# Two decode layers on one Trainium2 core: gate and up as rows, mean taken off late, joint score steps of two kv heads, w_down in six loads, new orders

## The chip, the cores and the metric

The kernel runs on one core of a Trainium2 chip. A core has a matrix engine (TensorE; PE in the profile, PEld where it loads weights), a vector engine (VectorE, DVE), a scalar engine (ScalarE, ACT), GpSimd (POOL) and SyncE (SP), which here only issues transfers. Each engine runs its own instruction list in order and waits on semaphores. Operands lie in SBUF (128 partitions), matmul results in eight banks of PSUM. 16 DMA engines fetch from HBM. The metric is the device time of one execution in microseconds (us), taken as the median of several; less is better.

## The reference

One pass over four tokens (B = 4, one position each) computes attention, feed-forward, attention, feed-forward, and both layers use the same weights and the same K and V cache:

```python
x = A_x                                                        # [4, 1, 448]
x = x + _A_ref(_layernorm(x), A_k_cache, A_v_cache, A_wq, A_wo)
x = x + _B_ref(_layernorm(x), B_w_gate, B_w_up, B_w_down)
x = x + _A_ref(_layernorm(x), A_k_cache, A_v_cache, A_wq, A_wo)
x = x + _B_ref(_layernorm(x), B_w_gate, B_w_up, B_w_down)

# _A_ref: 16 query heads, 8 kv heads, head size 256, the last W = 2048 of 8192 keys
q = (x @ wq).reshape(B, 1, 16, 256).transpose(0, 2, 1, 3)
scores = einsum("bhqd,bhkd->bhqk", q, k) * 256 ** -0.5
out = (softmax(scores) @ v).transpose(0, 2, 1, 3).reshape(B, 1, 4096) @ wo
# _B_ref: 448 -> 1792 -> 448
out = (silu(x @ w_gate) * (x @ w_up)) @ w_down
```

All data are bf16. The window of one token and kv head is 1 MB of K and 1 MB of V (2048 x 256), so the cache that is read measures 4 x 8 x 2 MB = 64 MB for one layer; the weights are 12.2 MB.

## The kernel before, in words

**Recording and orders.** `build()` records every operation into a graph (`g.op`, `g.dma`), with its engine, its emitting function, and the names it reads and writes. The order on each engine doesn't follow from this recording: it is written out in lists of operation numbers, `SEQ_PE`, `SEQ_DVE`, `SEQ_ACT`, `SEQ_POOL` and `SEQ_SP` (a "w" in SEQ_PE is a filler matmul that computes nothing needed, L1214). `schedule()` applies the lists and places the semaphore waits that the dependencies need.

**Loads.** All loads stand on SP's queue in the order of SEQ_SP. K and V arrive in halves of 512 KB (a pair of K halves can be one load of 1024 KB); `SLOTS` gives each half one of 31 places in SBUF, with seven more in the space of wq after the last q projection. A load whose place is still in use waits on SP for the PE operation that last reads the place, and everything behind it on SP waits too. Of a token's eight heads, six K and six V are held in their places from layer 0 to layer 1 (`KEEP_K`, `KEEP_V`) and not loaded again. L942 and L944 issue K, L958 issues V, L555 issues weights.

**Groups.** `PLAN` lists the work in steps; "202+203" is a group of two kv heads, heads 2 and 3 of token 2 in layer 0 (token, layer, head). A group runs over the engines: DVE transposes each K half (L948); PE makes the scores of both heads (L982); DVE takes the maximum (L995); PE spreads it (L1000, L1003); ACT takes exp (L1013); PE turns the probabilities (L1026) and ACT copies them (L1035); PE sums them (L1043); PE multiplies by V (PV, L1057, four operations of eight matmuls for the two heads and two V halves); POOL (L1070), ACT (L1072) and DVE (L1074) scale; PE flips the result (L1080) and DVE writes it to one of two buffers `oT` (L1090). The output projection with wo adds each head's part in PSUM, as rows (L1110) or, for the last heads of a token, as columns (L1102). Three steps of PLAN hold two groups, four heads ("002+003 004+005"): with two oT buffers, heads 2 and 3 of such a step are overwritten by 4 and 5 before their out projection.

**Hand-over of a token.** After a token's eight heads of layer 0, its rows are copied and turned (ACT L857, DVE L859, PE L867), the residual is added (L849, L877), and `norm()` gathers the mean and the variance (L586, L599, with DVE L589, L604, L606 and a chain of small POOL operations up to L622). `ffn()` computes gate and up (L785) as columns: 14 x 4 blocks of 128 x 128 of each weight matrix stand in PE, and x is broadcast to 32 columns, so each takes 56 matmuls. Then come tanh (ACT L805), three DVE operations (L808, L810, L817) and down (L826, 56 matmuls). After the second residual and a second norm, `qproj()` makes q of layer 1 (L671, 32 matmuls), ACT scales and copies (L677), PE turns (L687), DVE expands (L694), PE spreads (L701), DVE copies to qc (L706) and POOL makes the group's stationary operand qe (L987). Then the scores of layer 1 for the held heads can run, after them their PV; these free the places that SP waits for. A token in `LATE` or `QLATE` (only token 3 before) starts gate, or the q projection, from the raw x, and its mean is taken off afterwards by a matmul with the weights' column sums (L800, or in the turn).

## Time and profile before

| what | value |
|---|---|
| three runs: lowest, median, highest | 283.07, 284.09, 286.08 us |
| profiled execution: span | 283.0 us |
| around the span | the median is 1.1 us above the span |
| PE busy | 210.4 us (74%) |
| DVE busy | 168.6 us (60%) |
| POOL, ACT busy | 77.2 us (27%), 50.9 us (18%) |
| HBM read | 96.05 MB |
| mean granted TensorE clock | 0.895 |

In the profile's rows L12 is line 12 of the kernel. A row of a timeline gives start, busy time, engine, line, operation, what is written and read, and the number of instructions; in brackets the idle time before it and what ended it. A row of waits gives the waiting engine and line, the releaser, the total, the number and the longest. The slices cut the span into 40 equal parts.

### The profile page before, as it was taken

Reading aid. Unit: us, or ns where it says so; the run is one execution under the profiler, and the core shown is the slowest. Engines: PE = TensorE matmul, PEld = TensorE weight load, DVE = VectorE, ACT = ScalarE, POOL = GpSimd, SP = SyncE. Lnnn points to the kernel's source line nnn. Section 1 sums busy time; section 2 is a strip of 40 time slices with the busy share of each in tenths; the row PEclk is TensorE's granted clock in tenths of the full one; section 3 lists DMA queues with packets and bytes.
Section 4 is the critical chain, followed back from the end, with each engine's and each line's share of the span. In section 5 each row is a group of like instructions: output and inputs, shape, how many; then the busy total and the mean of one; then the engine's idle time right before and its main releaser. Section 6 shows DMA issues by size and latency. Waiting matters only on the chain.

```text
span 283.0 us, 9526 instructions
## 1 busy us (share of the span) xinstructions
PE 210.4 (74%) x4204; PEld 120.8 (43%) x4204; DVE 168.6 (60%) x511; ACT 50.9 (18%) x123; POOL 77.2 (27%) x202
## 2 busy tenths in 40 slices
...
DMA  6999999999999999968799999948799997899300
GB/s 258 424 414 401 413 410 402 407 401 406 377 390 408 400 408 406 409 278 307 290 324 403 411 406 408 397 170 295 254 316 412 415 405 266 286 341 415 125 2 3
DMA packets 27752, 96.67 MB, mean 342 GB/s; under 512 B 2747, under 2 KB 6847, under 8 KB 26431
## 3 DMA queue, kind: packets, MB, share of 16 engines
...
q8 instruction: 33, 0.54, 0.8%
...
q10 hardware_dynamic: 8, 0.00, 0.0%
HBM read 96.05 MB, written 0.00 MB: 339 GB/s over the span
## 4 chain that ended last, share of the span: by engine, by line
DMA 30%; PE 27%; SPq 23%; DVE 12%; issue 3%; ACT 3%; POOL 0%
DMA half<-in_A_k_cache_dram 13%; DMA half<-in_A_v_cache_dram 11%; SPq L555 10%; DVE half L948 8%; SPq L958 8%; DMA wd_sb<-in_B_w_down_dram 6%; PE A L1214 5%; PE Y L1057 5%; PE S L982 4%; PE Z L785 3%; SPq L944 3%; SPq L942 3%; PE Z L826 2%; PE A L1110 2%; DVE oh L1074 1%
## 5 line engine op out<-in xcount | busy, mean ns | idle before, releaser
L948 DVE STREAM_TRANSPOSE half<-half 128x1024 uint32<-128x1024 uint32 x80 | 98.0, 1233 | 16.3 <-DMA half<-in_A_k_cache_dram 15.9
L1214 PE MATMUL A<-identb,small 128*128 128x512 bf16 x147 | 51.0, 452 | 7.4 <-DVE A L478 5.5
L1070 POOL TENSOR_TENSOR small<-small 128x4 f32<-128x4 f32 x32 | 32.4, 1015 | 68.0 <-DVE small L1048 61.7
L982 PE MATMUL S<-half,qe 128*8 128x256 bf16 (+1 forms) x1040 | 40.8, 305 | 12.0 <-DVE half L948 11.1
L1057 PE MATMUL Y<-half,pT 128*8 128x256 bf16 x1024 | 42.2, 296 | 7.3 <-DMA half<-in_A_v_cache_dram 3.9
L982 PEld LDWEIGHTS S<-half,qe 128*8 128x8 bf16 x1040 | 25.4, 92 | 26.1 <-DVE half L948 15.5
L987 POOL TENSOR_TENSOR qe<-qc,tiny 128x64 bf16<-128x64 bf16 x64 | 17.2, 292 | 60.1 <-PE S L982 46.4
L1013 ACT ACTIVATE praw<-S,small 104x256 bf16<-104x256 f32 x32 | 15.1, 473 | 81.7 <-DVE small L1009 81.2
L1057 PEld LDWEIGHTS Y<-half,pT 128*8 128x8 bf16 x1024 | 22.2, 90 | 17.8 <-DMA half<-in_A_v_cache_dram 5.3
L995 DVE TENSOR_REDUCE tiny<-S 104x1 bf16<-104x256 f32 x32 | 13.3, 418 | 19.0 <-PE S L982 19.0
L1072 ACT ACTIVATE oh<-Y 128x256 bf16<-128x256 f32 x32 | 12.3, 383 | 66.3 <-PE Y L1057 61.9
L1214 PEld LDWEIGHTS A<-identb,small 128*128 128x128 bf16 x147 | 13.0, 109 | 20.4 <-issue 7.4
L1074 DVE SCALAR_TENSOR_TENSOR oh<-oh,small,Y 128x256 bf16<-128x256 bf16 x32 | 15.0, 468 | 11.0 <-ACT oh L1072 10.4
L1110 PE MATMUL A<-wo_sb,oT 128*4 128x448 bf16 x220 | 17.2, 380 | 0.8 <-DVE oT L1090 0.6
L1080 PE MATMUL Y<-tiny,oh 128*128 128x4 bf16 x64 | 6.6, 172 | 15.1 <-DVE oh L1074 15.0
L1048 DVE TENSOR_REDUCE small<-Y 128x4 f32<-128x64 f32 x32 | 7.0, 218 | 13.8 <-PE Y L1043 12.1
L1026 PE MATMUL Y<-selt,praw 104*64 104x48 bf16 x256 | 10.1, 197 | 5.9 <-ACT praw L1013 5.5
L1080 PEld LDWEIGHTS Y<-tiny,oh 128*128 128x128 bf16 x64 | 4.2, 103 | 22.5 <-DVE oh L1074 19.6
L1035 ACT ACTIVATE pT<-Y 128x192 bf16<-128x192 f32 x32 | 10.5, 329 | 15.6 <-PE Y L1026 15.3
L1026 PEld LDWEIGHTS Y<-selt,praw 104*64 104x64 bf16 x256 | 6.7, 113 | 12.6 <-ACT praw L1013 9.9
L671 PE MATMUL Z<-half,xn 128*5 128x512 bf16 x160 | 10.2, 379 | 2.2 <-DVE st L606 0.8
L612 POOL TENSOR_SCALAR st<-st 128x1 f32<-128x1 f32 x16 | 4.4, 274 | 26.4 <-DVE st L606 26.4
(125 smaller groups left out, 219.7 us busy)
## 6 DMA issues: line engine op xcount, KB each, us to landing
half<-in_A_v_cache_dram SPq DMA_DIRECT2D x80, 512.0 KB, 12.1
...
wg_sb<-in_B_w_gate_dram SPq DMA_DIRECT2D x1, 1344.0 KB, 17.3
...
```

Source lines behind the costliest of these rows:

```text
L555: g.dma(rank, nbytes, lambda e: e.dma_start(dst, src), f"w{nw[0]}", w=key if isinstance(key, tuple) else (key,), run=run)
L948: return e.transpose(a, a)
L958: g.dma(pp + VLAG, 1 << 19, lambda e, cell=cell, hv=hv, vsrc=vsrc: e.dma_start(unit(cell), vsrc[hv]), None, w=(f"v{t}_{kvh}_{hv}",), run=4 ...
L982: last = e.matmul(Sb[s_][qd:qd + 8, c0:c0 + rhs.free_size()], lhsT=qe[q_][:, P, ce, :, :].rearrange("p a n -> p (a n)"), rhs=rhs, start=(c ...
L987: g.op(POOL, 0.25, pos - SLEAD - 1, lambda e, P=P, t=t, kvh=kvh: e.tensor_tensor(qe[q_][:, P, :, :, :], qc[t][:, kvh, :, :].unsqueeze(2).b ...
L1013: return e.activation(praw[0:R, 0:128 * n].rearrange("p (g r l) -> p g r l", g=2 * n, l=2), Sb[s_][0:R, 0:128 * n].rearrange("p (l g r) -> ...
L1026: last = e.matmul(Yb[p_][64 * h:64 * h + 64, c0:c0 + (48 if n == 2 else 32)], lhsT=praw[0:R, 64 * gg:64 * gg + 64], rhs=w, start=(gg == 0) ...
L1057: last = e.matmul(Yb[p_][32 * gg:32 * gg + M, 256:512], lhsT=pT[pt][:, gg, 2 * a + hv, 4 * P:4 * P + M] if n == 2 else p1[:, gg % 2, 2 * a ...
L1070: g.op(POOL, 0.69, pos, lambda e: e.tensor_tensor(ri[p_][:, 0:2 * n], rs[p_][:, 0:2 * n], expo[:, 1:1 + 2 * n], op=ALU.pow), r=(f"rs{p_}", ...
L1074: g.op(DVE, 0.43, pos, lambda e: e.scalar_tensor_tensor(out=oh[:, :], in0=oh[:, :], scalar=lomask[:, 0:1], in1=Yb[p_][:, 256:512], op0=ALU ...
L1110: last = e.matmul(Ab[32 * k:32 * k + B, 0:D], lhsT=oT[oi][:, k % 2, k // 2, :], rhs=wo_sb[:, 4 * kvh + k, :], start=False, stop=False, ski ...
L1214: return e.matmul(Ab[:, 0:512], lhsT=zero[:, 0:1].broadcast_to([128, 128]), rhs=identb[:, :].unsqueeze(1).broadcast_to([128, 4, 128]), sta ...
```

## The change

Parts of the change:

1. **Gate and up as rows.** x (one or two columns) now stands in PE and the weights move: 16 matmuls per matrix with 448 weight columns each, in four column groups of 32 rows. The rows of gate are copied out of PSUM by ACT (448 columns), those of up by ACT and DVE (224 each), and five small matmuls per matrix turn them back to columns. The hidden units stand in a new order, and w_down is loaded to match.
2. **Mean off late** for tokens 1, 2 and 3, in gate and up and in q. The scale of q moves from ACT's copy to the DVE operation that expands.
3. **Direct qe.** Where a token's first layer-1 group follows its q projection with nothing between in that PSUM bank (in the new order tokens 0 and 2), DVE makes qe straight from it, instead of the copy to qc and POOL's product.
4. **Steps of two heads.** The three steps of four heads become two steps each, so heads are no longer overwritten. Code for a group of one head, and its seven small DVE operations at the start, goes, as do an unused row form of the whole FFN.
5. **w_down in six loads** (four of 128 x 3 x 448, two of 128 x 448), 1568 KB together as before.
6. **New orders.** All five SEQ lists and SLOTS are replaced. SP issues the same bytes. PE has 113 fillers, 147 before. Scores stay one operation for both heads.

```diff
-ROWF = ()
-LATE = ((3, 0),)
-QLATE = (3,)
+LATE = ((1, 0), (2, 0), (3, 0))
+QLATE = (1, 2, 3)
+PRE = (0, 1, 2)
 PLAN = (
-    "000+001", "002+003 004+005", "006+007", "100+101", "012+013", "014+015", "016+017", "102+103", "104+105",
+    "000+001", "002+003", "004+005", "006+007", "100+101", "012+013", "014+015", "016+017", "102+103", "104+105",
     "106+107", "200+201", "010+011", "115+113", "116+112", "114+117", "202+203", "204+205", "206+207", "300+301",
-    "212+213 214+215", "216+217 302+303", "306+305", "304+307", "110+111", "210+211 316+313", "314+315",
+    "212+213", "214+215", "216+217", "302+303", "306+305", "304+307", "110+111", "210+211", "316+313", "314+315",
     "312+317", "310+311",
 )
 SEQ_PE = (
-    "53 w w 57 w w w 60 w w w 68 w w 71 79 w 82 w 90 w w 93 w w 103 106 104 107 109 110 112 w w w w w 138 140 w w w w "
...
+    "46 50 53 61 64 w 72 75 83 86 96 99 97 100 102 103 w 105 136 173 138 175 141 210 143 w 212 178 145 180 341 146 247 "
...
-            load(rank_d, 1605632, wd_sb[:, :, :], B_w_down.rearrange("(c p) n -> p c n", p=128), "wd", 430)
+            for j in range(4):
+                load(rank_d, 344064, wd_sb[:, 3 * j:3 * j + 3, :], B_w_down[448 * j:448 * j + 384, :].rearrange("(c p) n -> p c n", p=128),
+                     f"wd{j}", 430)
+            wd_e = B_w_down.rearrange("(x h q) n -> x h q n", x=2, h=2)
+            for x in range(2):
+                load(rank_d, 114688, wd_sb[:, 12 + x, :], wd_e[x, :, 384:448, :], f"wd{4 + x}", 430)
...
+            if one:
+                vec(rank, lambda e: e.scalar_tensor_tensor(
+                    out=qS[:, 0:128].rearrange("p (c y) -> p c y", c=4),
+                    in0=Zb[:, 0:32].unsqueeze(1).broadcast_to([128, 4, 32]), scalar=st[:, ts[0], 8:9],
+                    in1=qone[:, :].unsqueeze(2).broadcast_to([128, 4, 32]), op0=ALU.mult, op1=ALU.mult),
+                    ("z", "qone", f"st{ts[0]}r2"), ("wa",), 0.25, ("Z",))
...
                 for cc in range(c0, c1):
-                    for fc in range(NFC):
+                    for j in range(4):
                         if cc < 3:
-                            lhsT, x = w[:, cc * FF + fc * 128:cc * FF + fc * 128 + 128], xn[:, cc, sl]
+                            lhsT, c = xn[:, cc, sl], cc * FF + 448 * j
                         else:
-                            lhsT = w[:, 3 * FF + (fc % 7) * 128:3 * FF + (fc % 7) * 128 + 128]
-                            x = xe[:, fc // 7, sl]
-                        last = e.matmul((Zb, Z2)[gi][:, k * m * fc:k * m * fc + k * m], lhsT=lhsT,
-                                        rhs=x.unsqueeze(2).broadcast_to([128, k, m]),
-                                        start=(fc == 0 and cc == 0), stop=(cc == 3), skip_group_check=True)
+                            lhsT, c = xe[:, j // 2, sl], 3 * FF + 448 * (j % 2)
+                        last = e.matmul(zb[32 * j:32 * j + k, 0:448], lhsT=lhsT, rhs=w[:, c:c + 448],
+                                        start=(cc == 0), stop=(cc == 3), skip_group_check=True)
+                return last
+
+            def turn(e, gi):
+                last, src = None, 512 * gi
+                o = zbs[gi][:, 0:NFC * k].rearrange("p (f t) -> p f t", t=k)
+                for c in range(4):
+                    for h in ((0,), (0, 1))[c == 3]:
+                        w_, f0, st_ = (128, c, 3) if c < 3 else (64, 12, 1)
+                        js = slice(0, 4) if c < 3 else slice(h, 4, 2)
+                        f1 = f0 + (10 if c < 3 else 2)
+                        last = e.matmul(o[64 * h:64 * h + w_, f0:f1:st_, :],
+                                        lhsT=wideb[:, src + 128 * c:src + 128 * c + w_], rhs=idn[:, js, 0:k],
+                                        start=(c == 0), stop=True, skip_group_check=True)
...
+            g.op(SCA, 0.54, rank, lambda e: e.activation(wideb[:, 0:448], Zb[:, 0:448], ACT.Copy), r=("z",), w=("wa",), bank=("Z",))
+            g.op(PE, 0.16, rank, lambda e: turn(e, 0), r=("wa", "identb"), w=("z",), bank=("Z",))
+            g.op(SCA, 0.31, rank, lambda e: e.activation(wideb[:, 512:736], Z2[:, 0:224], ACT.Copy), r=("z2",), w=("wb",), bank=("Z2",))
+            vec(rank, lambda e: e.tensor_copy(wideb[:, 736:960], Z2[:, 224:448]), ("z2",), ("wb2",), 0.31, ("Z2",))
+            g.op(PE, 0.16, rank, lambda e: turn(e, 1), r=("wb", "wb2", "identb"), w=("z2",), bank=("Z2",))
...
+                if t in PRE and layer == 1 and ahead[t][0] == gi and fresh[0] == (t, g.writer["z2"]):
+                    vec(pos, lambda e, P=P, kvh=kvh: e.tensor_tensor(
+                        qe[q_][:, P, :, :, :],
+                        Z2[:, 16 * kvh:16 * kvh + 16].rearrange("p (c h) -> p c h", h=2).unsqueeze(2).broadcast_to([128, 8, 4, 2]),
+                        qmask[:, :].unsqueeze(1).unsqueeze(3).broadcast_to([128, 8, 4, 2]), op=ALU.mult),
```

On PE, the hand-over of token 2 to layer 1. Before, from the last PV of the token (L1057) over the flip (L1080), the wo columns (L1102), scores of another group (L982), the norm's matmuls (L599, L586), gate and up to down (L826):

```order
L1057 MATMUL Y<-half,pT_55 8x256 x32
L1080 MATMUL Y<-tiny,oh 128x4 x2
L1214 MATMUL A<-identb,small 128x512 x6
L1102 MATMUL A<-oT,wo_sb 128x1 x32
L982 MATMUL S<-half,qe 8x256 x32
L599 MATMUL Z<-st,small 128x2
L1000 MATMUL S<-small,identb 104x32
L1003 MATMUL S<-identb,tiny 104x32
L586 MATMUL Z<-xn,twice 128x1
L785 MATMUL Z<-xn,wg_sb 128x32 x56
L785 MATMUL Z<-xn,wu_sb 128x32 x56
```

The same place after (L1038 is PV, L848 the turn of the rows, L1060 the flip, L1082 the wo columns, L589 and L602 the norm, L750 gate and up, L762 the turning matmuls):

```order
L848 MATMUL Z<-tiny,wide 128x1 x8
L1175 MATMUL A<-identb,small 128x512 x2
L1060 MATMUL Y<-tiny,oh 128x4 x2
L1038 MATMUL Y<-half,pT 8x256 x8
L1082 MATMUL A<-oT,wo_sb 128x1 x32
L1038 MATMUL Y<-half,pT 8x256 x8
L589 MATMUL Z<-xn,twice 128x1
L750 MATMUL Z<-wg_sb,xn 1x448 x12
L602 MATMUL Z<-st,small 128x2
L750 MATMUL Z<-wg_sb,xn 1x448 x4
L750 MATMUL Z<-wu_sb,xn 1x448 x16
L762 MATMUL Z<-identb,wide 128x4 x3
```

The other group's scores no longer stand between the wo columns and gate; some of the PV of other groups does, and gate starts ahead of the norm's second matmul.

On SP, the first loads of the program. Before, with L555 for x and the weights, L944 and L942 for K (whole and by halves) and L958 for V:

```order
L555 DMA wo_sb<-in_A_x_dram 4x448
L555 DMA half<-in_A_wq_dram 128x4096
L944 DMA half<-in_A_k_cache_dram 128x4096
L555 DMA half<-in_A_wq_dram 128x4096
L958 DMA half<-in_A_v_cache_dram 128x2048
L555 DMA half<-in_A_wq_dram 128x2048
L555 DMA half<-in_A_wq_dram 128x4096
L942 DMA half<-in_A_k_cache_dram 128x2048 x2
```

After, with L553 for x and the weights, L924 and L922 for K and L938 for V (rows from the start; the other three loads of wq and one more of K follow before the first V):

```order
L922 DMA half<-in_A_k_cache_dram 128x2048
L924 DMA half<-in_A_k_cache_dram 128x4096 x2
L553 DMA wo_sb<-in_A_x_dram 4x448
L922 DMA half<-in_A_k_cache_dram 128x2048
L924 DMA half<-in_A_k_cache_dram 128x4096
L922 DMA half<-in_A_k_cache_dram 128x2048 x4
L924 DMA half<-in_A_k_cache_dram 128x4096
L553 DMA half<-in_A_wq_dram 128x4096
L922 DMA half<-in_A_k_cache_dram 128x2048
L924 DMA half<-in_A_k_cache_dram 128x4096
L922 DMA half<-in_A_k_cache_dram 128x2048
L924 DMA half<-in_A_k_cache_dram 128x4096
```

The four loads of wq, which stood within the first seven loads, now stand behind ten and more loads of K, and x is no longer the first.

On SP around w_down, before (wg_sb and wu_sb are w_gate and w_up, wd_sb is w_down) and after:

```order
L555 DMA wg_sb<-in_B_w_gate_dram 128x3x1792
L555 DMA wu_sb<-in_B_w_up_dram 128x896
L555 DMA wu_sb<-in_B_w_up_dram 128x3x1792
L555 DMA wg_sb<-in_B_w_gate_dram 128x896
L555 DMA wd_sb<-in_B_w_down_dram 128x14x448
L958 DMA half<-in_A_v_cache_dram 128x2048 x2
L942 DMA half<-in_A_k_cache_dram 128x2048
```

```order
L553 DMA wd_sb<-in_B_w_down_dram 128x3x448
L938 DMA half<-in_A_v_cache_dram 128x2048
L553 DMA wg_sb<-in_B_w_gate_dram 128x3x1792
L553 DMA wu_sb<-in_B_w_up_dram 128x3x1792
L553 DMA wd_sb<-in_B_w_down_dram 128x3x448 x3
L938 DMA half<-in_A_v_cache_dram 128x2048 x2
L922 DMA half<-in_A_k_cache_dram 128x2048 x14
```

The last three parts of w_down stand behind w_gate and w_up as the one load did; behind them, where halves of V and K alternated, two halves of V and then 14 of K follow.

220 lines of the change are left out of this document (74 added, 146 removed), and 125 rows, old and new, of tables (SEQ_ACT, SEQ_DVE, SEQ_PE, SEQ_POOL).

## The prediction

> **What bounds the kernel now.** I read the page's slices first, to see which resource is full and where it is not.
>
> ```profile
> DMA  6999999999999999968799999948799997899300
> GB/s 258 424 414 401 413 410 402 407 401 406 377 390 408 400 408 406 409 278 307 290 324 403 411 406 408 397 170 295 254 316 412 415 405 266 286 341 415 125 2 3
> ```
>
> Each digit or number is a fortieth of the 283.0 us of span, 7.1 us. The DMA engines are full nearly everywhere, and three dents stand in the GB/s row: slices 18 to 21, 27 to 30 and 34 to 36. The busy times by stretch put sizes on them (the last two columns are DMA share and GB/s; PEclk is the one before).
>
> ```profile
> 0.00:10.00 10.00, 2.14 (x10) 0.88 (x11) 8.29 (x74) 0.00 (x0) 0.81 (x9) 1.00 0.78 308
> 120.00:150.00 30.00, 24.71 (x589) 16.00 (x590) 17.39 (x50) 5.41 (x13) 9.77 (x26) 1.00 0.81 304
> 150.00:180.00 30.00, 23.14 (x397) 11.88 (x396) 20.38 (x53) 5.95 (x16) 7.36 (x18) 0.89 1.03 409
> 180.00:213.00 33.00, 26.24 (x623) 17.26 (x623) 21.54 (x57) 6.90 (x17) 10.43 (x28) 0.95 0.79 278
> 230.00:252.00 22.00, 17.41 (x421) 11.44 (x424) 14.26 (x45) 4.07 (x9) 4.94 (x15) 1.00 0.86 304
> 252.00:266.00 14.00, 12.60 (x330) 8.12 (x319) 11.57 (x38) 4.71 (x12) 5.84 (x14) 1.00 0.87 348
> 266.00:283.00 17.00, 13.76 (x313) 8.89 (x310) 5.96 (x35) 3.14 (x9) 5.89 (x15) 0.77 0.01 3
> ```
>
> Fed, the queue moves 409 GB/s (150 to 180), so a half of 0.524 MB takes 0.524 / 0.409 = 1.28 us. Measured against that rate, the stretches lose 10 x (1 - 308/409) = 2.5 us at the start, 30 x (1 - 304/409) = 7.7 in what I call gap A, 33 x (1 - 278/409) = 10.6 in gap B, 22 x (1 - 304/409) = 5.6 in gap C, and 14 x (1 - 348/409) = 2.1 where the queue drains. The 96.67 MB of the page at 409 GB/s are 236.4 us; with these 28.5 and the 17 us without transfers they make 281.9 of the 283.0. So the kernel is bound by its loads, and what can be had is in the gaps and in the tail.
>
> The waits of SP, whose queue issues the loads in order, say what the gaps are.
>
> ```profile
> SPq L958 <- PE Z L599: 30.8, 2, 15.9
> SPq L958 <- PE Z L586: 29.5, 3, 14.6
> ```
>
> Each gap is the hand-over of a token to layer 1: L599 and L586 are matmuls of a layernorm that stand right behind the scores of held heads; SP waits for what those scores free. The load list shows the restart.
>
> ```profile
> 126.95 0.33 SPq L958 DMA_DIRECT2D half<-in_A_v_cache_dram  x1
> ...
> 143.97 1.22 SPq L942 DMA_DIRECT2D half<-in_A_k_cache_dram  x2
> ...
> 187.24 0.33 SPq L958 DMA_DIRECT2D half<-in_A_v_cache_dram  x1
> ...
> 201.96 0.33 SPq L958 DMA_DIRECT2D half<-in_A_v_cache_dram  x1
> ```
>
> **The change, gap by gap.** A gap is a race. The token's last V lands; from there PE, DVE and ACT need a chain of work until layer 1's first scores end and slots come free; SP meanwhile has some loads whose slots are free already: the cover. In gap B the chain reads on PE so:
>
> ```profile
> 181.62 1.05 PE L1057 MATMUL Y<-half,pT 128*8 128x256 bf16 x32
> ...
> 185.03 0.94 PE L1102 MATMUL A<-oT,wo_sb 128*128 128x1 bf16 x32
> 186.09 1.12 PE L982 MATMUL S<-half,qe 128*8 128x256 bf16 x32
> ...
> 187.98 1.55 PE L785 MATMUL Z<-xn,wg_sb 128*128 128x32 bf16 x56
> 189.38 1.55 PE L785 MATMUL Z<-xn,wu_sb 128*128 128x32 bf16 x56
> ...
> 191.20 1.56 PE L826 MATMUL Z<-wide,wd_sb 128*128 128x32 bf16 x56
> ...
> 193.22 0.61 PE L1057 MATMUL Y<-half,pT 128*8 128x256 bf16 x16 [0.39 <-DVE small L1048]
> ...
> 195.73 1.25 PE L671 MATMUL Z<-half,xn 128*5 128x512 bf16 x20 [0.29 <-DVE xn L589]
> ...
> 198.77 0.24 PE L701 MATMUL Z<-wide,fold 128*32 128x128 bf16 x4 [0.65 <-DVE wide L694]
> ...
> 200.03 3.55 PE L982 MATMUL S<-half,qe 128*8 128x256 bf16 x64 [0.70 <-POOL qe L987]
> ```
>
> The PV of the token's last group starts at 181.62; its V had landed before. That V stands six halves ahead of the last load issued before 187.24, and the queue runs dry there near 186.5, so I put its landing at 186.5 - 6 x 1.28 = 178.7, an estimate. The first 32 of the 64 scores end when SP goes on, at 201.96. The chain is 23.3 us.
>
> What the change does to it. **Rows for columns**: gate and up leave PE from 2 x 1.5 to two runs of 16 matmuls with 448 columns. The nearest row is the q projection: 20 matmuls of 512 columns in 1.25 us with the same column groups, so 16 are 1.0 us at most, 2.0 for both. But Z must now be copied, turned and only then used.
>
> ```profile
> L857 ACT ACTIVATE wide<-A 128x448 bf16<-128x448 f32 x8 | 4.3, 543 | 12.5 <-PE A L1110 12.5
> ```
>
> A turn is five small matmuls, by the four of 198.77 some 0.3 us. Copy 0.54 and turn 0.3 stand behind the up matmuls in part: gate's copy runs beside up's matmuls, up's own two half copies take 0.3 each on two engines. So gate to tanh goes from 3.0 to 2.0 + 0.3 + 0.3 = 2.6, a gain of 0.4; bounds: a loss of 0.5 (both copies exposed at 0.54) to a gain of 1. **Mean off late** for tokens 1 and 2: the gate matmuls need no longer wait for the norm that stands between 187.14 (scores end) and 187.98, 0.8 us, nor the q projection for the second one (192.8 to 194.5 and 0.29 at 195.73, of which 0.6 was PV work): 1.0. **Scores moved**: the 32 scores at 186.09 stand ahead of the wo columns now, 1.1 us off the chain, and 16 of the PVs, 0.6. **Direct qe**: L706 and the POOL product after it are one DVE operation for tokens 0 and 2: from 198.77 + 0.24 to 200.03 there are 1.0 us, of which 0.3 to 0.5 stay: 0.6. The fillers and the idle time before the wo columns (182.67 to 185.03, against flip, oT and ACT, DVE work of about 1.4) give about 1, and the scores before PV at the head 1 to 2. Sum: 23.3 - 0.4 - 0.8 - 1.0 - 1.1 - 0.6 - 0.6 - 1 - 1.5 = 16.3; I take 14.7 to 16.3. The new cover is 11 halves, 14.1 us (before 14, but a load in the middle waited too, at 187.24). The rows of the V loads' line bound what a restart adds.
>
> ```profile
> DMA to landing us min/median/max: 3.2/12.1/18.9
> ```
>
> 3.2 us is a load that found an idle queue, 1.9 of them before its own 1.28 of transfer; with half a microsecond for SP's issue and a ragged refill I count 2.4. Loss is then chain + 2.4 - cover = 3.0 to 4.6, and up to 7 if the chain saves only half. I take 4.3 for 10.6, **-6.3**.
>
> Gap A goes by the same working: mean off late (0.8 + 1.0), the 32 scores that end as SP goes on at 126.95 moved ahead of the last PVs, where they also let SP go on early, and the shorter head: chain 24.3 (from 119.7, found in the same way, to 143.97) to about 20.5, cover 17 halves, 21.8 us. Loss 20.5 + 2.4 - 21.8 = 1.1; I take 1.3, up to 3.3 if nothing but the moved scores is saved, for 7.7: **-6.4**. Token 1's first group still goes over POOL.
>
> Gap C: token 3 had its mean off late before, so only the head is shorter; its q projection ends at 246.66 + 1.06, 17.3 us after the last V lands (PE takes it up at 230.51, both below), and 14.8 now, cover 12 halves, 15.4. Loss 14.8 + 2.4 - 15.4 = 1.8, I take 2.2 for 5.6: **-3.4**; from -5 to 0.
>
> **A new small gap, 0.** Token 0's hand-over had its cover before. The first two rows are the chain of before, the third is the load that the scores behind it release:
>
> ```profile
> 64.22 17.12 DMA wd_sb<-in_B_w_down_dram
> 81.39 1.56 PE Z L826 x56
> ```
>
> ```profile
> 91.04 0.80 SPq L958 DMA_DIRECT2D half<-in_A_v_cache_dram  x2
> ```
>
> w_down's last part stands at 33.1 MB of the load order now, 31.0 before: 2.1 / 0.409 = 5 us later, 86.4. Behind it there are 7 halves (9.0 us) until one waits for layer 1's scores of token 0, 11 before. From the down matmuls to these scores it took about 9.5 us (81.39 to 91.04). Loss 9.5 + 2.4 - 9.0 = 2.9, less 0.6 for the direct qe: **+2.4**, from 0 to 5. The six parts carry what the one load did, to all partitions; beside an unchanged total I give them 0.
>
> The start is hidden. wq, wholly in by 14.2 MB where it was in by 5.3, lets the first scores begin near 48 us instead of 22 to 25, but SP has about 23 MB, 57 us, of loads ahead of the first that waits for a score, and DVE's transposes of K need no q. The seven small DVE operations that go were in an 8.29 us prologue without loads to wait for: 0.
>
> **The end.** The queue ends 6.3 + 6.4 + 3.4 - 2.4 = 13.7 us earlier, 265.9 to 252.2. But the PE is not idle there (12.60 of 14 us busy in the table). These pieces of the chain show the tail:
>
> ```profile
> 230.51 0.42 PE Y L1057 x8
> ...
> 246.66 1.06 PE Z L671 x16
> ...
> 275.53 0.30 ACT wide L805
> ```
>
> ```profile
> 268.72 1.05 PE L1057 MATMUL Y<-half,pT 128*8 128x256 bf16 x32
> ```
>
> Between the end of token 3's q projection (247.7) and that of the last PVs (268.72 + 1.05 = 269.8) PE fills 22.1 us. The q projection itself comes forward by 6.3 + 6.4 - 2.4 + 2.5 = 12.8, to 234.9, so PVs end at 257.0; the loads alone would allow 252.2 + 3.9 = 256.1. So 0.9 is given back. From there to the end the rest, 13.3 us, stays: gate in rows gains 0.3 at most, as tanh at 275.53 also waits for the POOL's pow.
>
> **The sum**: 283.0 - 13.7 + 0.9 - 0.3 = 269.9 of profiled span. The median of before, 284.09, is 1.1 above its span: 271.0. Every gap must come out as worked for that, and scatter only adds, so I say 272.
>
> L857's row gives 0.54 us for reading 448 columns out of PSUM, more than half of the 1.0 us in which PE writes them. The Trainium skill, "TensorEngine Tiling (Array Packing)", Performance Considerations, advises this swap with column tiling at 32 for few tokens, and warns in the same place that reading PSUM may then become the bottleneck. By the advice alone four chains would win 1 us each over columns, and the sum would be 270; by the warning it is rival 2.
>
> **The rivals.**
> 1. *Fewer fillers, slower clock.* 113 filler matmuls stand where 147 did. What the clock is worth shows at the end of gap B (PEclk third from the end):
>
> ```profile
> 200.10:203.40 3.30, 3.30 (x64) 1.98 (x64) 3.08 (x4) 0.00 (x0) 0.92 (x4) 0.50 0.54 190
> ```
>
> ```profile
> 251.89 2.05 PE L982 MATMUL S<-half,qe 128*8 128x256 bf16 x64
> ```
>
> At 0.50 the 64 scores took 3.55, at full clock 2.05. One such stretch of 3.3 us in each of three chains and one in the tail costs 4 x 1.5 = 6 us: 278. Against it: gaps A and C have 1.00, and the new chains hold denser work. The Trainium skill, "TensorE: Matmul & The Clock Gate", Part 1, tells of two speeds and a window of about 3.4 us; the trace agrees in both (0.50 or 1.00, 3.3 us here). What opens or shuts it no run here shows.
> 2. *The row form eats its gain.* Copies and turns are exposed on ACT and DVE, which in the gaps also hold exp, pT and the K transposes (1.23 us each, in order). If each of the four chains is 1.5 us longer than worked, three at the gaps and one in the tail: 272 + 6 = 278.
> 3. *The loads end early but PE does not.* The tail is PE's already; if the work left after the last V grows by what the gaps shifted, half of 13.7 comes back: 279. For it: 12.60 of 14; against it: 120 to 150 has only 24.71 of 30.
> 4. *Slower: the late start is not caught up.* From 48 us PE has two tokens of layer 0 in a heap. If token 0's last PV and wo are not done when w_down lands at 86.4, gap 0 grows one for one. It decides from the point where that eats the 12.1 us forecast and 2.8 more: token 0 ready 15 us late, at 101. At 20 us late: 292. For it: before, PE was waiting for w_down (L826 at 81.39), with computing from 22 on; now it has 26 us less. Against it: 38 us from 48 to 86 hold nine groups at 4 us of PE each (scores 2 x 1.1, PV 1.2 to 2, turns), and token 0 has four of layer 0.
> 5. *The gaps stay*: the scores that free slots wait for something else that comes last (a K transposed late by DVE, 1.23 us each), so the restart is no earlier. 282 to 285.
>
> **How the numbers follow.** Forecast 266 to 275: 0.55. Rivals 1 to 3 at 275 to 281: 0.22 together. Rival 5, 281.3 to 286.9 (1%, 2.8 us, is about what a measurement of this kernel can tell from no change): 0.09. Rival 4, above: 0.14. Faster 0.77, same 0.09, slower 0.14. The range takes in the bounds of the gaps (gap B at 7, gap A at 3.3, gap 0 at 5 add 7.3; the lower ends take 6 off) and rivals 1 to 3, and leaves out most of 4 and 5: 265 to 283.
>
> **What would show it.** The profile after should have about 304 to 380 GB/s in short dents where before there were three long ones, a first row near 400 GB/s and more, SP's longest wait below 8 us where it was 15.9, last loads landing near 252 and about 18 to 20 us behind them without transfers. A new dent at 86 to 97 us shows gap 0. ACT rows of about 0.54 us (448 columns) between gate and tanh show the row form's price; PEclk below 0.9 inside the hand-overs shows rival 1. If the GB/s row is low between 57 and 100 us, rival 4 is right and the forecast wrong.

## The result, and the profile after

The changed kernel takes 286.1 us (median of 20 runs, 283.34 to 288.18) where the kernel before, beside it on the same chip, takes 285.3 us (281.27 to 290.53). Executions over 1.5% above the fastest of their kernel are left out of the ratio, here and below; it is **1.011, 95% interval 1.007 to 1.014**: about 1% slower. The forecast was 272.0 us, 14 us away, and its range ended at 283; 286.1 lies in the range of rival 5 (281.3 to 286.9). The profiled executions are 283.7 us of span now and 283.0 before.

The row of slices of the page of after:

```profile
GB/s 246 408 412 424 422 410 377 370 364 400 391 389 330 265 215 410 407 413 406 241 358 342 414 407 405 409 408 393 163 326 410 412 407 262 317 353 411 122 2 3
```

Where the row before had three broad dents, this one has four narrow ones, and a dip in slices 7 to 9: the dents are cut down, not gone, and one is new (slices 13 to 15, about 85 to 106 us). The table by stretch, in the columns of before:

```profile
0.00:10.00 10.00, 0.26 (x4) 0.18 (x4) 7.60 (x44) 0.00 (x0) 0.81 (x9) 1.00 0.78 293
50.00:90.00 40.00, 27.55 (x445) 12.57 (x445) 7.83 (x39) 6.25 (x17) 7.15 (x13) 0.83 1.04 381
90.00:120.00 30.00, 23.13 (x483) 13.30 (x485) 22.34 (x51) 5.83 (x14) 8.51 (x21) 0.83 0.90 319
120.00:150.00 30.00, 25.63 (x502) 13.53 (x498) 14.34 (x56) 6.83 (x17) 7.04 (x17) 0.94 0.92 356
150.00:180.00 30.00, 23.84 (x462) 13.12 (x455) 25.11 (x55) 5.78 (x14) 10.51 (x30) 0.83 1.01 394
180.00:213.00 33.00, 28.75 (x620) 16.89 (x623) 23.09 (x69) 9.32 (x23) 10.56 (x25) 1.00 0.89 335
230.00:252.00 22.00, 19.33 (x376) 10.12 (x372) 14.41 (x50) 4.72 (x12) 5.97 (x14) 1.00 0.92 329
252.00:266.00 14.00, 11.73 (x301) 7.55 (x302) 10.15 (x35) 5.23 (x13) 8.09 (x20) 1.00 0.90 341
```

Two stretches of before that had not been shown:

```profile
50.00:90.00 40.00, 28.96 (x489) 15.29 (x493) 16.03 (x50) 4.95 (x11) 5.96 (x16) 0.83 1.04 397
90.00:120.00 30.00, 22.91 (x491) 12.73 (x483) 21.42 (x48) 6.84 (x17) 8.69 (x22) 0.94 1.03 406
```

Losses against 409 GB/s, in us, by the prediction's own formula:

| stretch | before | after | forecast after |
|---|---|---|---|
| 0 to 10 | 2.5 | 2.8 | 2.5 |
| 50 to 90 | 1.2 | 2.7 | 1.2 |
| 90 to 120 (gap 0) | 0.2 | 6.6 | 2.6 |
| 120 to 150 (gap A) | 7.7 | 3.9 | 1.3 |
| 150 to 180 | 0 | 1.1 | 0 |
| 180 to 213 (gap B) | 10.6 | 6.0 | 4.3 |
| 230 to 252 (gap C) | 5.6 | 4.3 | 2.2 |
| 252 to 266 | 2.1 | 2.3 | about 2 |

The three gaps gave 9.7 us instead of 16.1, and 9 us went back in gap 0 (6.4), between 50 and 90 us (1.5), and after gap A (1.1). The last load lands at 266.2 us, before at 265.8, and the tail behind it is 17.5 us, before 17.2. Four rows of the waits of SP:

```profile
SPq L922 <- PE Y L1038: 21.2, 8, 6.2
SPq L922 <- PE S L961: 19.5, 4, 7.8
SPq L938 <- PE S L961: 16.1, 4, 12.9
SPq L938 <- PE Z L589: 15.7, 2, 11.2
```

They are waits for scores (L961) and for PV (L1038) now more than for the norm behind the scores, and the longest is 12.9 us, not under 8. Of the other signs that were named, the new dent is there, the last landing near 252 us and the first row near 400 GB/s (293) are not; that the row is low from 85 us on was also a sign of rival 4, which e7 below tells apart from gap 0.

### The profile page after: what moved, and what is told of

It is laid out like the page before. It is cut to its first block, busy times and chain, and to the rows that moved or that the text cites. A ratio compares the mean times of both kernels' runs of the same rounds, so it can differ in the third digit from the quotient of the medians.

```text
span 283.7 us, 8746 instructions
## 1 busy us (share of the span) xinstructions
PE 199.3 (70%) x3808; PEld 107.7 (38%) x3808; DVE 170.9 (60%) x517; ACT 54.2 (19%) x133; POOL 75.5 (27%) x195
## 4 chain that ended last, share of the span: by engine, by line
DMA 41%; PE 29%; DVE 13%; SPq 10%; issue 4%; ACT 2%; POOL 0%; DVEq 0%; ACTq 0%
DMA half<-in_A_k_cache_dram 22%; DMA half<-in_A_v_cache_dram 14%; DVE half L928 8%; PE Y L1038 6%; PE S L961 5%; DMA wg_sb<-in_B_w_gate_dram 4%; SPq L938 3%; PE Z L750 3%; SPq L553 3%; SPq L922 2%; PE A L1090 2%; PE A L1175 2%; PE Z L807 2%; SPq L924 2%; PE Y L1011 2%
## 5 line engine op out<-in xcount | busy, mean ns | idle before, releaser
L928 DVE STREAM_TRANSPOSE half<-half 128x1024 uint32<-128x1024 uint32 x80 | 96.9, 1228 | 10.5 <-DMA half<-in_A_k_cache_dram 10.1
L1038 PE MATMUL Y<-half,pT 128*8 128x256 bf16 x1024 | 47.4, 298 | 13.9 <-DMA half<-in_A_v_cache_dram 10.7
L961 PE MATMUL S<-half,qe 128*8 128x256 bf16 x1024 | 39.3, 303 | 2.9 <-POOL qe L975 1.0
L1175 PE MATMUL A<-identb,small 128*128 128x512 bf16 x113 | 38.2, 392 | 0.4 <-DVE wide L840 0.4
L1038 PEld LDWEIGHTS Y<-half,pT 128*8 128x8 bf16 x1024 | 20.6, 90 | 29.0 <-DMA half<-in_A_v_cache_dram 14.3
L961 PEld LDWEIGHTS S<-half,qe 128*8 128x8 bf16 x1024 | 24.4, 91 | 12.4 <-DVE half L928 2.6
L1090 PE MATMUL A<-wo_sb,oT 128*4 128x448 bf16 x220 | 19.6, 382 | 4.8 <-DVE oT L1070 4.7
L615 POOL TENSOR_SCALAR st<-st 128x1 f32<-128x1 f32 x16 | 4.5, 282 | 56.2 <-DVE st L609 56.2
L602 PE MATMUL Z<-st,small 128*128 128x2 f32 x32 | 7.1, 291 | 17.3 <-DVE xn L592 12.9
L1070 DVE TENSOR_TENSOR oT<-Y,small 128x4 bf16<-128x4 f32 x64 | 8.2, 154 | 9.3 <-PE Y L1060 4.9
L602 PEld LDWEIGHTS Z<-st,small 128*128 128x128 f32 x32 | 5.8, 226 | 20.4 <-DVE xn L592 13.8
L1175 PEld LDWEIGHTS A<-identb,small 128*128 128x128 bf16 x113 | 9.3, 99 | 11.0 <-issue 8.9
L1117 POOL MEMSET oT<- 128x16 bf16 x28 | 3.0, 111 | 36.4 <-PE A L1090 21.4
## 6 DMA issues: line engine op xcount, KB each, us to landing
half<-in_A_k_cache_dram SPq DMA_DIRECT2D x7, 1024.0 KB, 16.3
wu_sb<-in_B_w_up_dram SPq DMA_DIRECT2D x1, 1344.0 KB, 15.4
```

The source lines that it names most:

```text
L602: g.op(PE, 0.45, rank, lambda e: e.matmul(Z2[:, 0:2], lhsT=onesf[:, 0:1].broadcast_to([128, 128]), rhs=s[:, 0:2], start=True, stop=True, s ...
L928: return e.transpose(a, a)
L961: last = e.matmul(Sb[s_][qd:qd + 8, c0:c0 + rhs.free_size()], lhsT=qe[q_][:, P, ce, :, :].rearrange("p a n -> p (a n)"), rhs=rhs, start=(c ...
L1038: last = e.matmul(Yb[p_][32 * gg:32 * gg + 8, 256:512], lhsT=pT[pt][:, gg, 2 * a + hv, 4 * P:4 * P + 8], rhs=unit(vss[P][hv])[:, 1024 * a ...
L1090: last = e.matmul(Ab[32 * k:32 * k + B, 0:D], lhsT=oT[oi][:, k % 2, k // 2, :], rhs=wo_sb[:, 4 * kvh + k, :], start=False, stop=False, ski ...
L1175: return e.matmul(Ab[:, 0:512], lhsT=zero[:, 0:1].broadcast_to([128, 128]), rhs=identb[:, :].unsqueeze(1).broadcast_to([128, 4, 128]), sta ...
```

## The experiments

A line such as `ahead(SEQ_PE, "651", "530")` puts operation 651 ahead of 530 in PE's list; numbers are operations, names are in the text. Ratios are to the kernel before; the changed kernel stands at 1.011 (1.007 to 1.014).

### Which wait holds gaps A and C

In gap A the token's own chain was not the last. DVE, PE and SP of after, around the restart:

```profile
136.57 1.24 DVE L928 STREAM_TRANSPOSE half<-half 128x1024 uint32<-128x1024 uint32 x1
...
137.91 1.23 DVE L928 STREAM_TRANSPOSE half<-half 128x1024 uint32<-128x1024 uint32 x1
...
139.19 1.10 PE L961 MATMUL S<-half,qe 128*8 128x256 bf16 x32
...
140.35 2.07 SPq L938 DMA_DIRECT2D half<-in_A_v_cache_dram  x2
```

L928 is the transpose of a K half, L961 the scores, L938 the issue of V. The scores at 139.19 are those of head 1 of token 0 in layer 1. That head's two K halves land at 136.3 and 137.6, *behind* token 1's last V (135.1); DVE transposes them, the scores run, SP goes on. The first transpose begins as DVE ends the scaling of token 1's last group (at 136.65), so K that lands earlier would still stand behind that on DVE's list. The first of token 1's own layer-1 scores end at about 154.3, 19.3 us after its last V as forecast (20.5), with loads at hand until about 160. In gap C it is the same with K of head 1 of token 1 (lands at 235.8, SP goes on at 238.50, ahead of the end of token 3's own chain).

**e1_k_early** loads these K halves ahead of the last V halves and moves transposes and scores with them; **e2_weights_early** puts two V halves behind w_down to bring it forward; **e3_both** has both.

```diff
+SEQ_SP = ahead(SEQ_SP, "643 645".split(), "516")     # e1: K (0,1,1) ahead of V (1,0,7)
+SEQ_DVE = ahead(SEQ_DVE, "644".split(), "539")
+SEQ_DVE = ahead(SEQ_DVE, "646".split(), "534")
+SEQ_PE = ahead(SEQ_PE, "651".split(), "530")
+SEQ_SP = ahead(SEQ_SP, "1208".split(), "1110")       # e1: K (1,1,1) ahead of V (3,0,4)
+SEQ_DVE = ahead(SEQ_DVE, "1209".split(), "1102")
+SEQ_PE = ahead(SEQ_PE, "1214".split(), "1131")
+SEQ_SP = ahead(SEQ_SP, "331 332".split(), "337")     # e2: V (1,0,0) behind w_down
+SEQ_PE = ahead(SEQ_PE, "350 351".split(), "352")
```

> Edit: of token 0's and token 1's first layer-1 group, the K halves that were loaded behind the last V of token 1 and of token 3 are loaded ahead of it, and their transposes and scores stand ahead of that PV. Theory W (the load queue stops not for the token's own chain but for scores of another group whose K came last): SP's wait that ends at 140.35 in the changed kernel ends near 137.6, the one at 238.50 near 236.0; the 5 us lost at 120 to 160 become 2 to 3 and the 6 us at 230 to 266 become 4 to 5; time 3 to 5 us below the changed kernel, so 0.993 to 1.000 of the kernel before. Rival R (a stop costs the same wherever it falls, and the token's chain is next): no more than 1 us, 1.007 to 1.012 of the kernel before.

> Edit: two V halves of token 1 that stood ahead of w_gate, w_up and the last parts of w_down are loaded behind them, and their PV stands behind down. Theory G (gap 0 is the late weights and the short cover behind them): w_down is complete 2.6 us earlier (near 87.8, 90.38 in the changed kernel), two more halves cover the chain, SP's wait that ends at 99.02 ends near 97, and of the 6.6 us lost at 90 to 120 some 4 come back; 0.995 to 1.000 of the kernel before. Rival (the two PV that now come late hold up the loads that wait for their places and token 1's work): nothing comes back, 1.008 to 1.014 of the kernel before.

> Both edits, of the early K and of the early weights. If W and G hold and the gaps are separate, the gains add: 6 to 9 us below the changed kernel, 0.980 to 0.990 of the kernel before, with the last load landed near 258 to 260 instead of 266. If a gain at one gap is taken back at the next, no more than the better of the two alone.

Measured: e1 1.030 (1.023 to 1.037), e2 1.010 (1.007 to 1.014), e3 1.019 (1.013 to 1.026). In e1 SP goes on at 138.9, earlier, but stands again for the PV of held groups in both gaps, and the last V's come later. Gap C of e1 and the stretch in which it stands:

```profile
230.00:252.00 22.00, 19.24 (x342) 9.90 (x338) 9.94 (x39) 3.67 (x10) 5.43 (x12) 0.84 0.81 289
242.00:249.00 7.00, 6.93 (x101) 3.53 (x101) 3.51 (x17) 1.76 (x5) 2.52 (x6) 0.52 0.49 176
```

289 GB/s where after has 329, at a granted clock of 0.84, and 0.52 in the second stretch, where after has 1.00 throughout. In e2 the two moved PV became what the next loads wait for, and gap 0 lost more, not less (299 GB/s). So the wait that was named is real (in e1 it ends 1.5 us earlier), and shortening it uncovers the next one.

### What a stop of the queue costs

**m1_restarts** leaves out all computing and only loads, in six batches with an empty queue between them, in one execution; a V batch and the only batch of 1 MB loads are shown.

> Measures a stop of the load queue by itself: no computing, six batches of 5 MB each into SBUF, each started some 5 us after the last one has landed in full: V halves (twice), K halves, whole K of 1 MB, V halves, and V halves while VectorE transposes all the time. Theory F (a restart itself is ragged): after a stop the ten halves need 3.5 + 9 x 1.28 + 2 or more = 17 us from issue to the last landing, in every batch. Rival (the queue refills cleanly and what was ragged in the kernel comes from what runs beside it): 15 to 15.5 us in the quiet batches, and more only in the last one.

Ten V halves, and then five K loads of 1 MB, from the issue of the first (columns: DVE, POOL, PEclk, DMA share, GB/s):

```profile
22.90:26.90 4.00, 0.00 (x0) 0.00 (x0) 1.00 0.77 265
26.90:30.90 4.00, 0.00 (x0) 0.00 (x0) 1.00 1.02 391
...
66.30:70.30 4.00, 0.00 (x0) 0.00 (x0) 1.00 0.67 252
70.30:74.30 4.00, 0.00 (x0) 0.00 (x0) 1.00 1.00 422
```

Ten halves took 15.8 to 16.3 us from the first issue to the last landing, the same 5.2 MB in five loads 14.8; at 409 GB/s it is 12.8. So a stop costs 3.0 to 3.5 us beyond its wait with loads of 512 KB, 2.0 with 1 MB, where the formula had 2.4. With halves the third load landed 2.1 to 2.8 us behind the second instead of 1.28, in each of the batches of halves; with 1 MB loads this step is missing. A busy VectorE made no difference (15.8). The Trainium skill, "DMA: Bandwidth & Descriptors", Bandwidth, advises to batch transfers to 1 MiB or more; the batches agree, for the refill (14.8 against 15.8 to 16.3 us).

In the kernel a restart takes longer than in m1. After SP goes on in gap 0, at 99.02, these are the rows of after (last column GB/s):

```profile
98.00:100.00 2.00, 2.00 (x65) 1.59 (x58) 2.00 (x4) 0.00 (x0) 1.09 (x4) 1.00 0.23 78
100.00:102.00 2.00, 1.51 (x37) 1.02 (x39) 2.00 (x4) 0.47 (x1) 0.70 (x4) 1.00 0.81 227
102.00:104.00 2.00, 1.50 (x48) 0.95 (x40) 1.90 (x6) 1.02 (x3) 0.54 (x2) 1.00 0.86 252
104.00:106.00 2.00, 1.99 (x53) 1.10 (x49) 1.71 (x5) 0.47 (x1) 1.90 (x2) 1.00 0.93 219
```

They lose 4.2 us against 409 GB/s, although SP went on 0.75 us before the last load issued earlier had landed (99.77). Counted like m1, from SP's issue to the landing of the tenth half, less 10 x 1.28, the restart is 5.6 us in gap 0, 5.2 in gap A and 5.3 in gap B, and it was 5.5 in before at 201.96. By the bytes moved it is 4.5 in gap B (the 6.0 lost there, less the 15.6 of chain, plus the 14.1 of cover). So the formula's 2.4 is some 5 us in this kernel; m1 accounts for 3.0 to 3.5 of it, and where the rest comes from stays open. Where SP goes on earlier, this is hidden: in before's gap 0 it went on at 91.04, with loads landing until 95.4, and 0.2 us were lost.

### Row form and mean off late

**e4_columns** takes gate and up back to columns and drops copies and turns; **e5_norm_first** makes gate and q of tokens 1 and 2 wait for the mean again and puts the norm's matmuls ahead of them.

```diff
-lhsT, c = xn[:, cc, sl], cc * FF + 448 * j
-last = e.matmul(zb[32 * j:32 * j + k, 0:448], lhsT=lhsT, rhs=w[:, c:c + 448],
+last = e.matmul(zb[p0:p0 + wd_, k * m * f:k * m * f + k * m], lhsT=w[:, c + o:c + o + wd_],
+                rhs=x.unsqueeze(2).broadcast_to([128, k, m]),          # e4
...
-rn = tuple(f"xn{t}" for t in ts) + ("xone",)
+rn = tuple(f"xn{t}" for t in ts) + ("xone",) + tuple(f"st{t}m" for t in ts if t in (1, 2) and not last)   # e5
```

> Edit: in the changed kernel, gate and up as columns again (x broadcast to 32 columns, 64 matmuls per matrix for the new hidden order), without the copies out of PSUM and the turns; everything else, the orders too, as changed. Theory A (the row form moves time about but hardly saves any): in the changed kernel's trace gate to down takes 3.8 us for token 2 and 4.7 at the end, in the kernel before 3.2 and 5.2; with columns token 2's hand-over is up to 0.6 shorter and the tail up to 0.5 longer, the whole within 1 us of the changed kernel: 1.006 to 1.015 of the kernel before. Rival 1 (the rows save 1 us per hand-over): 2 to 4 us slower than the changed kernel, 1.018 to 1.025. Rival 2 (the copies are the bottleneck): 2 us faster, 1.000 to 1.005.

> Edit: gate and the q projection of tokens 1 and 2 wait for the mean of their norm again, and the norm's matmul stands ahead of them; the mean is still taken off afterwards. Theory M (late mean shortens a hand-over by 1 to 1.8 us, which counts only where that hand-over ends the stop of the load queue, in gap B): SP's wait that ends at 203.64 ends 1 to 1.8 later; token 1's makes no difference; 1 to 2 us slower than the changed kernel, 1.013 to 1.018 of the kernel before. Rival (PE has other work to put there, so nothing is lost): 1.007 to 1.012.

Measured: e4 1.043 (1.035 to 1.052), e5 1.036 (1.025 to 1.048): 9 and 7 us over the changed kernel, more than either theory. SP goes on in gap B at 208.4 in e4 and 211.1 in e5, against 203.64. In this order both parts are gains, then, but not at this price by themselves: the order was made for them, and the clock was lower here too (0.66 and 0.83, where after has 1.00). What the chain and what the clock cost is not told apart. Ten microseconds of gap B of e4, then of e5:

```profile
195.00:205.00 10.00, 9.15 (x193) 6.11 (x189) 4.64 (x20) 1.25 (x3) 2.53 (x8) 0.66 0.68 254
```

```profile
195.00:205.00 10.00, 8.73 (x174) 5.10 (x172) 4.48 (x27) 1.56 (x4) 1.68 (x6) 0.83 0.79 285
```

### The clock

**e10_no_fillers** drops the 113 filler matmuls; **e7_wq_first** restores the early start.

```diff
+SEQ_PE = [x for x in SEQ_PE if x[0] not in "wq"]              # e10
+HELD = ["0"] * len(HELD)
+SEQ_SP = ahead(SEQ_SP, "41 42 43 45 44".split(), "130")       # e7: x and wq first
```

> The changed kernel without its 113 filler matmuls, everything else in the same order. Theory K (the hand-overs hang on the granted clock): the mean clock falls from 0.92 to under 0.86, half-clock stretches fall into the hand-overs of gaps 0, A, B or C, the queue resumes 1 to 4 us later there, and the ratio is 1.025 to 1.06. Rival (fillers cost as much as they give): 1.000 to 1.015.

> Edit: in the changed kernel x and the four loads of wq come first again, ahead of all K. The first scores can run near 20 us, not 45. Theory S (the late start is hidden, since V and the weights land when they do): SP's waits stay within 1 us, 1.005 to 1.013 of the kernel before. Rival (work heaped up behind the late start is why token 0's hand-over and the loads between 50 and 110 are late): 3 to 6 us come back, 0.990 to 1.000.

e10 took 293.5 to 300.0 us in four executions. The two that count in a ratio average 294.6, 3.5% above the 284.7 of the kernel before beside them, so some 2.4% or 7 us above the changed kernel; two are few. The profiled one has a span of 293.8 us, 10 more than after, at a mean clock of 0.789 instead of 0.922. Gap A, and gap C with what surrounds it:

```profile
135.00:149.00 14.00, 10.94 (x172) 5.58 (x172) 6.00 (x22) 2.69 (x7) 3.20 (x8) 0.53 0.75 287
...
224.00:261.00 37.00, 32.10 (x494) 15.30 (x492) 17.54 (x58) 6.53 (x17) 7.75 (x18) 0.51 0.85 319
```

The same two stretches of after:

```profile
135.00:149.00 14.00, 13.19 (x282) 7.68 (x286) 7.29 (x34) 3.06 (x8) 3.77 (x9) 1.00 0.80 297
...
224.00:261.00 37.00, 32.92 (x671) 17.72 (x670) 21.98 (x78) 9.12 (x23) 12.74 (x33) 1.00 0.96 353
```

So the fillers hold the clock in the hand-overs, and without them 7 to 10 us are lost. In the changed kernel gaps A, B and C have 1.00: rival 1 is not what happened, but every experiment that thins the work near a hand-over must be read with it. The Trainium skill, "TensorE: Matmul & The Clock Gate", Part 1, ties the lower clock to an idle window of about 3.4 us; e10 agrees in direction (0.789 against 0.922), e6 below does not in the length of the idle time (1.0 us at most).

e7 is at 1.007 (1.003 to 1.011), not told from the changed kernel: the late start is hidden, as forecast, and rival 4 falls.

### Taking the FFN out of a chain

**e6_no_ffn_2** leaves out token 2's layer-0 FFN, the middle of gap B's chain; **e8_no_ffn_2_filled** puts 15 fillers in its place.

```diff
+g.mute = t in (2,)                       # e6, e8: operations recorded here are dropped
 ffn(with_ + [t], pos, late, False)
+g.mute = False
+SEQ_PE, HELD = with_fill(SEQ_PE, HELD, 3, "869", 1)      # e8: n fillers ahead of an operation
+SEQ_PE, HELD = with_fill(SEQ_PE, HELD, 3, "877")
+SEQ_PE, HELD = with_fill(SEQ_PE, HELD, 5, "903")
+SEQ_PE, HELD = with_fill(SEQ_PE, HELD, 4, "914")
```

> Leaves out token 2's feed-forward of layer 0 (gate, up, tanh, down), so the output isn't the reference's; orders and loads as changed. Its chain from the last V to layer 1's scores gets some 5 us shorter, 15.6 to about 10.5, less than the 14.1 us of loads behind the last V. Theory B (a stop of the queue costs its wait and its restart, and without the wait both go): no stop near 203, of the 6.8 us lost there 5 to 7 come back, 0.984 to 0.993 of the kernel before. Rival (other waits stand right behind the one that goes, as in the run with early K): 1 to 3 us come back, 0.999 to 1.007.

> Token 2's layer-0 FFN is left out (the output is not the reference's, as in e6_no_ffn_2), and 15 filler matmuls stand in its place on TensorE, in the hand-over of gap B. In e6_no_ffn_2 the load queue resumed at 204.58 as before, with a granted clock of 0.50 from 195 to 205; there the 28 projection matmuls took 3.16 us and 64 of the scores 3.23 us. Theory K (the clock ate what the left out FFN freed): the granted clock is above 0.9 in 190 to 205, the queue resumes 2.5 to 4 us earlier than in e6 (200.5 to 202), before the cover ends at about 202, gap B's loss falls from 6.8 to under 3 us, and the kernel stands at 0.985 to 1.000 of the kernel before. Theory N (the next wait holds the queue, whatever the clock): the queue again stands until 203 to 205 and the ratio stays at 1.005 to 1.015. If the wait closes and the ratio still stays over 1.005, then what gap B gives is lost later.

e6 is at 1.014 (1.006 to 1.022): nothing came back, and SP went on at 204.3. Its clock fell in the very place:

```profile
185.00:190.00 5.00, 4.34 (x82) 2.25 (x83) 1.87 (x8) 1.08 (x3) 1.01 (x1) 1.00 1.03 409
190.00:195.00 5.00, 3.38 (x59) 1.63 (x56) 2.31 (x11) 0.38 (x1) 1.68 (x6) 0.63 1.03 410
195.00:200.00 5.00, 4.92 (x45) 1.68 (x43) 3.54 (x12) 0.75 (x2) 1.30 (x4) 0.50 0.95 370
200.00:205.00 5.00, 4.09 (x66) 2.11 (x68) 2.80 (x7) 0.44 (x1) 1.20 (x5) 0.50 0.08 33
```

TensorE is busy 4.34 of 5 us, then 3.38, as the clock falls (0.50 from 191.3 to 205.0 us); the longest idle piece between 180 and 200 us is 1.0 us. e8 keeps the clock at 1.00 there, and SP still goes on only at 203.8; 1.006 (1.001 to 1.011). So theory K fell. What stands in the FFN's place is on VectorE:

```profile
195.11 0.48 DVE L1073 SCALAR_TENSOR_TENSOR oh<-oh,small,Y 128x256 bf16<-128x256 bf16 x1 [0.65 <-ACT oh L1071]
195.51 1.25 DVE L947 STREAM_TRANSPOSE half<-half 128x1024 uint32<-128x1024 uint32 x1
196.68 0.20 DVE L1089 TENSOR_TENSOR oT<-Y,small 128x4 bf16<-128x4 f32 x2
196.79 0.14 DVE L615 SCALAR_TENSOR_TENSOR st<-xr,small 128x4 f32<-128x4 f32 x1
```

The second norm's first step (L615, at 196.79) could, by the profile, run soon after 194; in the fixed order it stands behind the scaling of a group whose V has just landed (L1073) and the transpose of a K half. The order had filled the FFN's time with such steps for later loads, and these hold the chain once the FFN is gone.

**e12_turns_late** moves transposes of that kind in the full kernel behind the projection's steps, and computes everything.

```diff
+SEQ_DVE = ahead(SEQ_DVE, "444".split(), "471")
+SEQ_DVE = ahead(SEQ_DVE, "1073 1036 1042".split(), "1207")
+SEQ_PE = ahead(SEQ_PE, "360".split(), "361")
```

> The changed kernel with four transposes of newly landed K halves put behind the steps of the projection that they stand in front of on VectorE: K (1,0,3) in gap 0, K (3,0,6), (3,0,2), (3,0,3) in gap B; the wo row of (1,0,0) goes behind token 0's scores. Everything is computed. In the changed kernel the qS copy of gap B stood behind a transpose until 201.43 with its input at about 200.5, and that of gap 0 until 96.75. If these transposes hold the hand-over, the queue resumes 0.8 to 1.5 us earlier in gap B (202.2 to 202.9 instead of 203.64) and 0.4 to 0.8 us earlier in gap 0, and the kernel comes to 1.001 to 1.007. Rival (the later transposes hold the next scores, and the next wait takes it): 1.008 to 1.016.

SP went on at 202.8 in gap B, 0.9 us earlier as expected, and the kernel became slower, 1.023 (1.014 to 1.033). Gap C paid:

```profile
230.00:252.00 22.00, 20.02 (x368) 10.14 (x368) 11.94 (x44) 4.84 (x13) 5.89 (x14) 0.92 0.77 273
```

273 GB/s where after has 329, 3.0 us. The K half that gap C waits for landed 1.3 us earlier than in after, and DVE began its transpose at 237.27 instead of 235.82, behind a scaling step (L1065, 236.87 to 237.35).

### A stop that is made shorter

**e9_no_ffn_0**, **e11_no_ffn_0b** and **e14_no_ffn_0c** leave out token 0's layer-0 FFN and column sums, so that nothing that SP waits for hangs on w_down. They differ in how PE is filled and in where the two PV of heads 0 and 1 of token 1, the next that SP waits for, stand.

```diff
+SEQ_PE = ahead(SEQ_PE, "352 353 357 360".split(), "361")   # e9, e11: PV, flip, row behind all scores
+SEQ_PE = ahead(SEQ_PE, "352 353".split(), "389")           # e14: PV behind the first scores
+SEQ_PE = ahead(SEQ_PE, "357 360".split(), "361")
+SEQ_DVE = ahead(SEQ_DVE, "356 444 359 358 471".split(), "607")
+SEQ_ACT = ahead(SEQ_ACT, "355".split(), "370")
+SEQ_PE, HELD = with_fill(SEQ_PE, HELD, 2, "314")           # e9, e14; e9 also 16 and 8 ahead of 352, 357
+SEQ_PE, HELD = no_fill(SEQ_PE, HELD, "286", "306")         # e11: none in the FFN's place, 8 ahead of 352
```

> Token 0's layer-0 FFN and the column sums that it makes for the late mean are left out (the output is not the reference's); w_gate, w_up and w_down are loaded as before. The PV of group (1,0,1), which stands ahead of token 0's scores in the changed kernel, is put behind them, with its copies; 26 filler matmuls take the place of the FFN. So nothing that the load queue waits for hangs on w_down any more. Theory S (the stops of the queue set the end): the stop at 99 us goes (loss there from 5.4 to under 1.5 us), nothing new stands in its place before 135 us, and the kernel is 3.5 to 5.5 us faster than the changed one: 0.991 to 0.999 of the kernel before. Theory N (what one stop gives back, the next takes): the stop goes, the later gaps grow, and the ratio stays between 1.003 and 1.015.

> As e9_no_ffn_0 (token 0's layer-0 FFN and its column sums left out, the output not the reference's; the PV of group (1,0,1) behind token 0's scores), but without the fillers that stood in the FFN, and with 8 instead of 26 new ones, since in e9 these held TensorE until 96.8 us and the moved PV came late. Theory S (a stop of the load queue costs the time that it takes): token 0's scores end by 91 us, the PV at 93 to 94, the queue never runs dry between 90 and 110 us (loss under 2 instead of 5.4 us), and the kernel is 3 to 5 us faster than the changed one: 0.993 to 1.001 of the kernel before. Theory N (what a stop gives back is taken by the later ones): the stop goes and the ratio is still 1.003 to 1.015, with gaps A, B and C larger than 4.3, 6.8 and 4.9 us.

> As e9_no_ffn_0 (token 0's layer-0 FFN and its column sums left out, the output not the reference's), with the two PV of group (1,0,1) right behind the first of token 0's scores instead of behind all of them, and without the 24 fillers that stood there; the fillers that stand in the changed kernel's FFN stay, since without them (e11) the clock fell to 0.50 and the PV came at 96.6 us again. Theory S: token 0's first scores end by 93.5, the PV by 94, the queue never runs dry between 90 and 110 us (loss under 2 instead of 5.4 us), and the kernel is 3 to 5 us faster than the changed one: 0.993 to 1.001 of the kernel before. Theory N: the stop goes and the ratio is still 1.003 to 1.015, with the later gaps larger than 4.3, 6.8 and 4.9 us.

SP's first issue after the wait, in e9, e11 and e14 (after: 99.02):

```profile
98.64 5.06 SPq L950 DMA_DIRECT2D half<-in_A_k_cache_dram  x10
```

```profile
98.43 5.01 SPq L956 DMA_DIRECT2D half<-in_A_k_cache_dram  x10
```

```profile
93.89 9.66 SPq L949 DMA_DIRECT2D half<-in_A_k_cache_dram  x11
```

In e9 and e11 the stop stayed, held by my own fillers in the one and by a clock of 0.74 in the other, and the times too: 1.010 (1.006 to 1.014) and 1.015 (0.996 to 1.035). In e14 SP goes on 5 us earlier, 3.1 us before the last load issued earlier lands, and it takes 282.5 us, **0.995 (0.991 to 0.999)**: 1.6% under the changed kernel, some 4.6 us. The stop is shorter, not gone: e14 has 353 GB/s between 90 and 120 us (after: 319), so 2.5 of the 6.6 us lost there came back, and the expected loss of under 2 was not reached. Of the profiled executions of e9 and e14 (296.3 and 287.2 us, the longest of their ten) only this early part is read. The same work is left out in all three, but besides the stop they differ in fillers, e9 having 24 more than e14, and in the clock. So theory S is supported by one run, and not more: a stop that gets shorter, with no other wait in its place and the clock kept until SP goes on, comes back at the end; how much of the 4.6 us is the stop is not settled.

### The small loads of w_down

**e13_small_early** and **e15_small_first** move the two 112 KB loads; **e16_small_by_half** cuts them by halves of the partitions; **e17_half_wq** is e16 with e7.

```diff
+SEQ_SP = ahead(SEQ_SP, "119 118".split(), "132")     # e13: at 24 us; e15: ahead of "327", at 2.5 us
...
-wd_e = B_w_down.rearrange("(x h q) n -> x h q n", x=2, h=2)
-    load(rank_d, 114688, wd_sb[:, 12 + x, :], wd_e[x, :, 384:448, :], f"wd{4 + x}", 430)
+wd_e = B_w_down.rearrange("(x h q) n -> h q x n", x=2, h=2)                       # e16, e17
+    load(rank_d, 114688, wd_sb[64 * h:64 * h + 64, 12:14, :], wd_e[h, 384:448, :, :], f"wd{4 + h}", 430)
```

> The changed kernel with the two small loads of w_down (112 KB, rows of 896 bytes) issued behind the first load of w_gate's second part, at 24 us, instead of at 33 and 47 us among the V halves and wo. If the small loads themselves cost the 1.5 and 3.1 us that the stream lost around them, the loss moves to 42 to 46 us with them and the time stays at 1.008 to 1.014. If it is their place (beside the loads of wo, whose rows are short too), the stream's loss before 65 us falls from 4.5 to under 2.5 us; the time then falls by under 1 us where the later gaps set it (1.007 to 1.011) and by 2 us where the bytes set it (1.002 to 1.006).

> The changed kernel with the two small loads of w_down (112 KB, rows of 896 bytes) as the fifth and sixth load of the program, where the queue holds nothing yet that the next load would wait for, instead of at 33 and 47 us. In the changed kernel the load behind each was issued late (42.95 and 52.90 us, 10.1 and 5.9 us after its turn), and in e13_small_early, with both in one place, at 41.67, and the DMA share fell to 0.48 there. If that is the cause of the early loss, the loss before 65 us falls from 4.5 to under 1.5 us, w_down is complete 2 to 4 us earlier (86.5 to 88.5 instead of 90.38), the whole sequence behind it moves up by as much, and the kernel comes to 0.995 to 1.003. Rival (the bytes of the early stage do not set the end, as in e7_wq_first): 1.005 to 1.013.

> The changed kernel with the last 128 rows of w_down's four blocks (224 KB) still in two loads of 112 KB at the same two places, but cut by halves of the partitions (64 partitions, two rows of 896 bytes each, a source of one regular step) instead of over all 128 partitions with a source in two parts. Everything is computed. In e13 and e15 the two loads lost the stream 4.1 us wherever they stood, so it is the loads themselves. If it is the form of the source over the partitions, the loss before 65 us falls from 4.5 to under 2 us, w_down is complete 2 to 4 us earlier than 90.38 us, and since e14 gave back at the end what it took from the stop at 99 us, the kernel comes to 0.996 to 1.003 of the kernel before. If it is the short rows or the small size, the loss stays at 4 to 5 us and the ratio at 1.006 to 1.013.

> The two edits that were not slower than the changed kernel and compute everything, together: the small loads of w_down by halves (e16) and x and wq loaded first (e7). e16 had w_down complete 1.8 us earlier and the queue back 1.7 us earlier in gap 0 and 0.85 us in gap B; e7 had no stop of its own. If the early microseconds come back at the end, the kernel is 2 us under the changed one and level with or under the kernel before: 0.996 to 1.003. If the stops B and C take them, as e16's profile says (its last V landing at 266.6 us as in the changed kernel), it stays at 1.004 to 1.011.

The stretches in question, of before, after (10 to 20 and 40 to 65), e13, e15 (both stretches) and e16:

```profile
40.00:65.00 25.00, 18.33 (x233) 7.79 (x227) 10.38 (x25) 3.66 (x9) 3.07 (x6) 0.74 1.03 404
```

```profile
10.00:20.00 10.00, 0.78 (x3) 0.61 (x3) 9.35 (x32) 0.00 (x0) 1.64 (x5) 1.00 1.02 409
40.00:65.00 25.00, 16.81 (x302) 8.44 (x294) 7.94 (x23) 5.75 (x12) 5.85 (x14) 0.81 1.03 375
```

```profile
40.00:65.00 25.00, 19.61 (x306) 9.59 (x294) 7.95 (x23) 5.85 (x12) 6.04 (x15) 1.00 1.00 370
```

```profile
10.00:20.00 10.00, 0.62 (x4) 0.50 (x2) 5.40 (x26) 0.00 (x0) 0.00 (x0) 1.00 0.98 353
40.00:65.00 25.00, 19.25 (x304) 10.12 (x304) 8.82 (x29) 5.38 (x11) 8.63 (x23) 1.00 1.03 400
```

```profile
40.00:65.00 25.00, 16.35 (x302) 8.50 (x290) 7.93 (x23) 5.56 (x12) 5.74 (x13) 0.80 1.04 372
```

The dip goes where the two loads go: e15 has 400 GB/s at 40 to 65 and the dip at 10 to 20, where it loses 10 x (409 - 353)/409 = 1.4 us; in the old place it is 25 x (400 - 375)/409 = 1.5 us. So the two loads cost about 1.5 us of stream beyond the 0.56 us of their 0.23 MB, and neither the place (e13 1.007, 1.001 to 1.013; e15 1.006, 1.002 to 1.010) nor the cut (e16 1.010, 1.005 to 1.015) takes it away. My expectations had 4.1 us, from landing times, which follow the order in which loads finish and overstate it; the bytes moved say 1.5. In e16 w_down was complete 1.8 us earlier and SP went on earlier in gap 0 (97.0) and gap B (202.5), and its last V landed at 266.6, as in after: gaps B and C took it.

e17 has a profiled span of 281.6 us, and a ratio of 1.008 (1.004 to 1.012): no version that computes everything beats the kernel before.

## Why the prediction was wrong, point by point

- **What bounds the kernel**: right. The sum over stretches still makes the span, and in e14 a shorter stop came back at the end.
- **The chains**: right. 15.6 us in gap B (forecast 14.7 to 16.3), 19.3 in A (20.5), 14.7 in C (14.8), 8.6 from w_down to SP in gap 0 (8.9). Gate to down in token 3's tail went from 5.15 to 4.72 us (forecast 0.3 less). The row form and the late mean help (e4, e5), though how much of their 7 to 9 us is chain and how much clock is not settled.
- **"[...] with half a microsecond for SP's issue and a ragged refill I count 2.4": the failing step.** The loss of a gap was chain + 2.4 - cover, and the 2.4 was built from the landing of one load that found an idle queue. Measured, it is some 5 us (4.5 to 5.6), in before too. With 5 for 2.4, and all else as forecast (in B with the measured chain), the formula gives 3.7 us in A (20.5 + 5 - 21.8), 6.5 in B (15.6 + 5 - 14.1), 4.4 in C (14.8 + 5 - 15.4) and 4.9 in gap 0 (8.9 + 5 - 9.0), together 19.5. Measured are 3.9, 6.0, 4.3 and 6.6, together 20.8, where 10.4 were forecast: 10.4 of the 14 us. This is worked out afterwards; no run changes the restart alone inside the kernel.
- **"The token's last V lands; from there [...] a chain of work": wrong in gaps A and C.** A gap was taken as one race, between one token's chain and a cover of "loads whose slots are free already". There the first load behind the cover waits for another group's scores, whose K was loaded behind the token's last V and still had to be transposed. That is rival 5's mechanism, given 0.09. It did not make the loss by itself: SP went on 5.3 us behind the last V in A and 4.0 in C, with covers of 6.3 and 5.0, so with 2.4 the formula would still have given 1.4 us in each, about as forecast, and with 5 it gives 4.0 in each. But mending that one wait could not have saved the forecast: e1, e6, e8 and e12 each shortened a wait or its chain and met the next, on SP's list, in VectorE's order, or in the clock.
- **Gap B** is the one place where the race was as pictured (SP on at 203.6; the cover ran to 202.0), and the restart alone was wrong: 6.0 instead of 4.3.
- **Gap 0**: the chain (8.6) and the cover (9.4, forecast 9.0) were right, the restart again not. w_down was complete at 90.4, not 86.4, as its estimate took the full rate from the load order, but the loads behind it came later with it. 6.6 instead of 2.6: 4.2 in the four rows above, and 1.3 ahead of the stop, between 90 and 94 us (250 and 309 GB/s), which the formula does not have.
- **"The six parts carry what the one load did [...] I give them 0"**: wrong by about 1.5 us (e15).
- **The start is hidden**: right (e7). **The end**: as in the sum, 17.5 us behind the last landing.
- The range rested on each gap's own bounds. They were bounds of the chains; the 2.4, which stood in all four gaps, had none, and 2.6 more in each is 10.4 us. That the same SP list holds several waits close behind one another was a rival of 9%.

What stays open: why a restart takes some 2 us more in the kernel than alone, why the third load after a stop comes late in m1, why the small loads cost what they do, and by what TensorE's clock falls in one thinned hand-over (e6, with no idle piece over 1.0 us) and not in another (e14, at 1.00 until 100.9 us, behind an idle piece of 3.9).
